# A bilinear feed-forward after sparse attention: two more pairs by seven products, another order at the end of a tile, banks by name

## The chip, the cores and the metric

The kernel runs on one core of a Trainium2 chip. The metric is the device time of one execution in microseconds. The engines are called as in the profile: PE multiplies matrices, PEld is its loading of weights, DVE, ACT and POOL work elementwise, SP issues transfers.

## The reference

```python
def _attn_ref(q, k, v):                     # q, k, v: (8, 8, 576, 64)
    scores = scale * np.matmul(q, k.transpose(0, 1, 3, 2))
    rel = pos[:, None] - pos[None, :]
    mask_local = (rel >= 0) & (rel < 32)
    mask_strided = (rel >= 0) & (pos[None, :] % 32 == pos[:, None] % 32)
    ...                                     # heads 0-3 local, 4-7 strided; softmax
    return np.matmul(attn, v)

def _moe_ref(x, w_a, w_b, w_out):           # x: 4608 x 512, w_a and w_b: 512 x 1536, w_out: 1536 x 512
    a = x @ w_a
    b = x @ w_b
    return (a * b @ w_out).astype(np.float32)

def reference(**kwargs):
    ...
    x = attn_out.transpose(0, 2, 1, 3).reshape(B * S, H * D)
    return _moe_ref(x=x, **moe_kwargs)
```

Only the second part, the feed-forward, is touched by the change. Its first projection is `a = x @ w_a` and `b = x @ w_b`, its second projection is `(a * b) @ w_out`.

## The kernel before

**Tiles and slots.** The 4,608 tokens are cut into nine tiles (`NT`, t = 0 to 8) of 512 (`TTOK`). Each tile has 16 slots: twelve for the blocks f of 128 columns of `d_ff` in the first projection (`ffn_ab`), then four for the second projection (`ffn_ys`, which draws 21 matmuls of a generator in each slot and the rest in the last). Blocks f = 2g and 2g + 1 are a pair; there are six pairs (`FG`), g = 0 to 5. The attention of the next batches is woven between these matmuls by `take`; the last of it is done within tile 6, so tiles 7 and 8 hold the feed-forward alone. Small works are hung on slots: `do(i, ...)` puts a call behind slot i, and the table `soon` does so ahead of `take(i)`. All five engines run in the order in which the program emits their instructions (`manual_schedule`).

**First projection, plain.** For one block f, `ab_mm` makes four matmuls of 512 columns for a and four for b (L626), each pair of banks from `mm_bank`. ACT copies a to `a_sb` (L647) and DVE multiplies it with b into `pf` (L650), as bf16.

**First projection, seven products.** For the pairs g listed in `FAST_A[t]` (in tiles 7 and 8), `a_pair` makes a of both blocks at once as a 2 x 2 block product by seven products instead of eight: the halves of the 512 contracted rows and the pair's two blocks on one side, the two halves of the tile's tokens on the other. The sums of weights (`wsum_make`) and of inputs (`xsum_make`) are made for all pairs ahead of time. Each product P("1") to P("7") is two matmuls of 256 columns (L703). Products 1, 6, 5, 3 accumulate in bank X, which ACT copies after each (L719, L722, L730, L738); 7 and 4 in bank Z, 2 in bank Y. ACT copies Z after product 7 (L725); DVE adds Y (L727) and Z (L736) to the quarters that they belong to, and POOL adds the copy of Z (L731). Between the products b is made plainly, four matmuls of 512 columns for each block (L710). `mult(1)` and then `mult(0)` multiply a with b for the odd and the even block (L715). The call is a generator with two parts, one for each of the pair's slots. X lies in the ring "st" for even g and "o" for odd g.

**Second projection.** In tiles 2 to 8 (`FAST_Y`) this is also made by seven products, with `pf` as the stationary side. `products(t)` says what each needs: product 1 the even blocks of `pf` and `w_out`, product 2 and 4 the odd blocks, 3, 5, 6 and 7 the differences s[0] to s[3] that `fast_s(t, n, gs)` makes from `pf` for the groups gs, n = 0 to 3 (L758, on DVE; product 6 needs n = 1, 7 needs n = 2, 5 needs n = 0, 3 needs n = 3, and n = 1 and 3 are made from n = 0 and 1). Each product is made for the two sets q = 0, 1 of tokens; a block such as "10" is product 1 for q = 0, six matmuls of 256 columns, one for each g. `Y_ORDER` (tiles 2 to 7, `y_plan`, L812) and `TAIL_ORDER` (tile 8, `y_tail`, L841) give the order of the 14 blocks. `y_post` takes a finished bank to `y_sb`: copies on ACT for products 1, 7, 6, 5 (L789) and 3 (L795), additions on DVE for 4 (L791) and 2 (L793), and one more on DVE after 5 (L787). In tile 8 the last block is cut in two halves of 128 columns, and `y_store` (L778) sends out the rows as they are done, five times through SP's queue and once through ACT's. In tile 7 the two stores (L807) hang on slots of tile 8.

**Tile 8's differences** are made group by group in the slots of its first projection. `fast_s` puts the difference n = 2 of a group off when this and the next pair are both in `FAST_A[8]`: `a_pair` of the next pair then makes it on POOL (`later`, L756, L733).

**Banks.** PSUM has eight: three in the ring "mm", one in "tp", and two each in "o" and "st". `mm_bank` counts its calls and takes "tp" at every fourth and "mm" otherwise; `a_pair` names its rings itself.

The order in time at the places that the change touches: pair 4 and pair 5 of tile 7, its second projection, pair 0 of tile 8, and so on up to pair 5 of tile 8, its second projection, and the last stores.

Of the kernel before, what the change touches and what calls it, by code (L numbers as in the profile page):

```python
# [7 lines left out]
F32 = mybir.dt.float32  # L8
# [16 lines left out]
VW = 128  # L25
WCH = (0, 2, 5, 9, 12)
FAST_Y = (2, 3, 4, 5, 6, 7, 8)
FAST_A = {7: (1, 2, 3, 4), 8: (0, 1, 2, 3, 4)}


@with_exitstack
def kernel(
# [571 lines left out]
    def take(pos):  # L604
        for b, names in steps.get(pos, ()):
            run(b, names)
# [5 lines left out]
    def mm_bank(shape):  # L612
        nm = "tp" if used[0] % 4 == 3 and used[0] >= 0 else "mm"
        used[0] += 1
        return psum4[nm].tile(shape, F32, tag=nm, name="mm")
# [65 lines left out]
    def a_pair(t, g):  # L681

        pf = pfs[t]
        pool, nm = ((pst, "st"), (psum4["o"], "o"))[g % 2]
        X = pool.tile([128, 2, 512], F32, tag=nm, name="ax")[:, 0, :HT]
        a = ([fsb.tile([128, TTOK], F32, tag="a_sb", name="a_sb") for _ in range(2)] if g % 2 == 0 else
             [t.rearrange("p h n -> p (h n)")[:, :2 * TTOK].bitcast(F32) for t in kT_buf[0]])
        got = {k: psum4[nm].tile([128, TTOK], F32, tag=nm, name="mm")
               for k, nm in zip((1, "Z", "Y", 0), (("mm", "mm", "tp", "mm"), ("tp", "mm", "mm", "mm"))[g % 2])}
        Z, Y = got["Z"][:, :HT], got["Y"][:, :HT]  # L690
        p7 = fsb.tile([128, HT], F32, tag="p7", name="p7")
        quarter = lambda e, k: a[e][:, HT * k:HT * (k + 1)]
        w = lambda e, j: (lambda c: wav[:, j, c, g, e])
        ws = lambda n: (lambda c: wsum_a[n][:, c, g])
        x = lambda j, k: (lambda c: x_part(t, j, k)[:, c])
        xs = lambda n: (lambda c: xsum[t][:, n, c])
        plan = {"1": (X, w(0, 0), x(0, 0)), "2": (Y, w(0, 1), x(1, 0)), "3": (X, ws(3), x(1, 1)), "4": (Z, w(1, 1), xs(3)),
                "5": (X, ws(0), xs(0)), "6": (X, ws(1), xs(1)), "7": (Z, ws(2), xs(2))}

        def P(k):  # L700
            bank, lhs, rhs = plan[k]
            for c in range(2):
                nc.tensor.matmul(bank, lhsT=lhs(c), rhs=rhs(c), start=k in "172" and c == 0, stop=c == 1, skip_group_check=True)  # L703

        x0 = TTOK * t % (XR * S)

        def b_mm(e, kks):
            f = 2 * g + e
            for kk in kks:
                nc.tensor.matmul(got[e], lhsT=wb_sb[:, kk, 128 * f:128 * (f + 1)], rhs=xT[:, kk, x0:x0 + TTOK],  # L710
                                 start=kk == 0, stop=kk == KD - 1)

        def mult(e):
            halves = lambda v_: v_.rearrange("p (a i s) -> p a i s", i=2, s=16)
            nc.vector.tensor_mul(pf[:, 2 * g + e, :].rearrange("p (i a s) -> p a i s", i=2, s=16),  # L715
                                 halves(a[e]), halves(got[e]))

        P("1")
        nc.scalar.copy(quarter(0, 0), X)  # L719
        b_mm(1, (0, 1, 2))  # L720
        P("6")
        nc.scalar.copy(quarter(1, 0), X)  # L722
        b_mm(1, (3,))
        P("7")
        nc.scalar.copy(p7, Z)  # L725
        P("2")
        nc.vector.tensor_tensor(quarter(0, 0), Y, quarter(0, 0), op=ALU.add)  # L727
        yield None
        P("5")
        nc.scalar.copy(quarter(1, 1), X)  # L730
        nc.gpsimd.tensor_tensor(quarter(1, 1), quarter(1, 1), p7, op=ALU.add)  # L731
        if (t, g - 1) in later:
            later.pop((t, g - 1))()  # L733
        b_mm(0, (0, 1))
        P("4")
        nc.vector.tensor_tensor(quarter(1, 0), Z, quarter(1, 0), op=ALU.add)  # L736
        P("3")
        nc.scalar.copy(quarter(0, 1), X)  # L738
        b_mm(0, (2, 3))
        mult(1)  # L740
        mult(0)
        yield pf[:1, 2 * g + 1, :1]

    later = {}
# [28 lines left out]
    def col(j):  # L773
        return slice(HN * j, HN * (j + 1))

    def y_store(eng, t, y, i, q, n=slice(0, d_model)):
        rows = out[TTOK * t:TTOK * (t + 1), n].rearrange("(a i s q) c -> a s i q c", i=2, s=8, q=2)
        eng.dma_start(out=rows[:, :, i, q], in_=y[i][:, q, n])  # L778
# [4 lines left out]
    def y_post(k, y, q, bank, n=slice(0, HN)):  # L783

        part = lambda i, j: y[i][:, q, HN * j:HN * (j + 1)]
        if k == "+":
            nc.vector.tensor_tensor(part(1, 1), part(1, 1), part(0, 1), op=ALU.add)  # L787
        elif k in "1765":
            nc.scalar.copy({"1": part(0, 0), "7": part(0, 1), "6": part(1, 0), "5": part(1, 1)}[k], bank)  # L789
        elif k == "4":  # L790
            nc.vector.tensor_tensor(part(1, 0), bank, part(1, 0), op=ALU.add)  # L791
        elif k == "2":
            nc.vector.tensor_tensor(y[0][:, q, n], bank, y[0][:, q, n], op=ALU.add)  # L793
        elif k == "3":
            nc.scalar.copy(part(0, 1), bank)  # L795

    Y_ORDER = [(x[0], int(x[1])) for x in "10 11 70 71 60 61 40 41 50 51 20 21 30 31".split()]
    TAIL_ORDER = [(x[0], int(x[1])) for x in "10 70 60 11 40 50 71 30 61 20 51 41 31 21".split()]

    def y_plan(t):  # L800

        plan, y = products(t), y_bufs()
        bank = {x: mm_bank([128, 2, HN]) for x in "ZXY"}

        def store_half(i):
            rows = out[TTOK * t:TTOK * (t + 1)].rearrange("(a i s q) c -> a s i (q c)", i=2, s=8, q=2)
            nc.sync.dma_start(out=rows[:, :, i], in_=y[i].rearrange("p q c -> p (q c)"))  # L807

        for n, (k, q) in enumerate(Y_ORDER):
            b, lhs, rhs = plan[k]  # L810
            for g in range(FG):
                nc.tensor.matmul(bank[b][:, q], lhsT=lhs(g, q), rhs=rhs(g), start=k in "172" and q == 0 and g == 0,  # L812
                                 stop=g == FG - 1, skip_group_check=True)
                if g == FG - 1:
                    if q == 1:
                        y_post(k, y, slice(0, 2), bank[b])
                        if k == "5":
                            y_post("+", y, slice(0, 2), None)
                    take(("y", t, n + 1))
                yield y  # L820
        do(16 * t + 19, store_half, 0)
        do(16 * t + 20, store_half, 1)

    def y_tail(t):

        plan, y = products(t), y_bufs()
        banks = [{x: mm_bank([128, HN]) for x in "ZXY"},
                 {"X": psum4["o"].tile([128, 2, 512], F32, tag="o", name="end")[:, 0, :HN],
                  "Z": pst.tile([128, 2, 512], F32, tag="st", name="end")[:, 0, :HN]}]
        for k, q in TAIL_ORDER:  # L830
            b, lhs, rhs = plan[k]
            cuts = [slice(0, HN)]
            if (q, k) == (1, "2"):
                cuts = [slice(0, 128), slice(128, HN)]
            for n in cuts:
                if (q, k) == (1, "2"):
                    bank = mm_bank([128, 128])
                else:
                    bank = banks[q][b]
                for g in range(FG):  # L840
                    nc.tensor.matmul(bank, lhsT=lhs(g, q), rhs=rhs(g)[:, n], start=g == 0 and k in "172",  # L841
                                     stop=g == FG - 1, skip_group_check=True)
                    if g < FG - 1:
                        yield y
                y_post(k, y, q, bank, n)
                if k == "5":
                    y_post("+", y, q, None)
                if k == "54"[q]:
                    y_store(nc.sync, t, y, 1, q)
                elif (q, k) == (0, "2"):  # L850
                    y_store(nc.sync, t, y, 0, q)
                elif (q, k) == (1, "3"):
                    y_store(nc.sync, t, y, 0, q, col(1))
                elif (q, k) == (1, "2"):
                    y_store(nc.scalar if n.start == 0 else nc.sync, t, y, 0, q, n)
                yield y

# [47 lines left out]
    with tc.manual_schedule(engines={ENG.PE, ENG.SP, ENG.Pool, ENG.DVE, ENG.Activation}):  # L905
# [88 lines left out]

        soon = {}
        for t in FAST_Y[:-1]:
            soon[16 * t + 10] = [lambda t=t: fast_s(t, 2, slice(4, 6))]
            soon[16 * t + 11] = [lambda t=t, n=n: fast_s(t, n, slice(4, 6)) for n in (0, 1)]
        do(0, fill_v, vl_buf[0])
        do(0, fill_v, vs_buf[0])  # L1000
# [40 lines left out]
        for n, slot in enumerate((16, 16, 19, 20)):  # L1041
            do(slot, fast_w, n, slice(3, 6))
        for g in range(FG):
            for n in (2, 0, 1, 3):
                do(16 * (NT - 1) + 2 * g + 1, fast_s, NT - 1, n, slice(g, g + 1))
        for t in FAST_Y[:-1]:
            for slot, n, z0, z1 in ((4, 0, 0, 2), (5, 2, 0, 2), (6, 1, 0, 2), (7, 3, 0, 2), (8, 2, 2, 4), (9, 0, 2, 4),
# [45 lines left out]
```

## Time and profile before

| | us |
|---|---|
| median of 3 runs | 325.69 (325.45 to 326.91) |
| the profiled execution | 325.6 |
| span of its profile, first to last instruction | 323.9 |
| tile 7, pair 0 (plain), 260.92 to 264.37 | 3.45 |
| tile 7, pairs 1 to 4 (seven products), 264.37 to 277.39 | 13.02 |
| tile 8, pair 0 (seven products), 290.03 to 293.51 | 3.48 |
| tile 8, pairs 1 to 4 (seven products), 293.51 to 306.53 | 13.02 |

The time of an execution lies 1.7 us above the span of its profile. In the rows of busy time by stretch, as the next section shows them, a row gives the stretch in microseconds from the span's start, its length, and then for PE, PEld, DVE, ACT and POOL the busy time and the number of instructions that lie in it, wholly or in part; the last three numbers are the granted clock of PE, the share of the DMA engines' time and GB/s. In the rows of the order of time, the first two numbers are the start and the length of a group of instructions, followed by engine, line, operation, what it writes and reads, the shape and the count; a bracket holds the idle time before and who ended it. A matmul's record is longer than its share of PE, since matmuls overlap; what counts is the distance from start to start.

### The profile page before, as it was taken

Reading aid. Unit: us, or ns where it says so; the run is one execution under the profiler, and the core shown is the slowest. Engines: PE = TensorE matmul, PEld = TensorE weight load, DVE = VectorE, ACT = ScalarE, POOL = GpSimd, SP = SyncE. Lnnn points to the kernel's source line nnn. Section 1 sums busy time; section 2 is a strip of 40 time slices with the busy share of each in tenths; the row PEclk is TensorE's granted clock in tenths of the full one; section 3 lists DMA queues with packets and bytes.
Section 4 is the critical chain, followed back from the end, with each engine's and each line's share of the span. In section 5 each row is a group of like instructions: output and inputs, shape, how many; then the busy total and the mean of one; then the engine's idle time right before and its main releaser. Section 6 shows DMA issues by size and latency. Waiting matters only on the chain.

```text
span 323.9 us, 7466 instructions
## 1 busy us (share of the span) xinstructions
PE 317.7 (98%) x2686; PEld 209.2 (65%) x2686; DVE 258.6 (80%) x560; ACT 189.4 (58%) x332; POOL 161.0 (50%) x291
## 2 busy tenths in 40 slices
PE   8999999999999999999999999999999999999994
PEld 6754655455555587557999885569555966686673
DVE  6766888888778899898888888988999768837952
ACT  6764775478764576447644764476546655335541
POOL 8935848599857554853576247634013012203500
PEclk9999999999999999999999999999999999999999
DMA  9999999999999989999999999999146040004004
GB/s 158 151 203 194 204 187 188 170 174 129 141 216 142 134 87 98 111 209 152 101 101 189 176 97 106 175 194 115 33 95 157 10 130 3 0 0 132 1 2 130
DMA packets 110724, 40.43 MB, mean 125 GB/s; under 512 B 88672, under 2 KB 107744, under 8 KB 110688
## 3 DMA queue, kind: packets, MB, share of 16 engines
q0 software_dynamic: 85968, 19.48, 67.0%
q1 hardware_dynamic: 24576, 20.42, 25.1%
q8 instruction: 21, 0.34, 0.5%
q14 instruction: 15, 0.12, 0.1%
q10 hardware_dynamic: 144, 0.07, 0.1%
HBM read 39.51 MB, written 10.91 MB: 156 GB/s over the span
## 4 chain that ended last, share of the span: by engine, by line
PE 95%; DMA 1%; ACT 1%; DVE 1%; issue 0%; SPq 0%
PE mm L626 46%; PE mm L812 17%; PE mm L876 6%; PE mm L710 5%; PE st L392 4%; PE o L470 2%; PE ax L703 2%; PE o L529 2%; PE mm L703 2%; PE mm L841 2%; PE end L841 1%; DMA raw<-in_q_dram 1%; PE misc L155 1%; PE ab L626 1%; PE tp L296 1%; PE tp L554 1%
## 5 line engine op out<-in xcount | busy, mean ns | idle before, releaser
L626 PE MATMUL mm<-xT,wa_sb 128*128 128x512 bf16 (+1 forms) x400 | 92.6, 353 | 0.0
L626 PE MATMUL mm<-xT,wb_sb 128*128 128x512 bf16 (+1 forms) x400 | 92.6, 353 | 0.0
L647 ACT COPY a_sb<-mm 128x512 f32<-128x512 f32 x88 | 51.4, 585 | 51.3 <-PE mm L626 49.3
L626 PEld LDWEIGHTS <-wb_sb 128*128 128x128 bf16 x408 | 39.4, 98 | 35.6 <-DMA wb_sb<-in_moe_w_b_dram 0.2
L1059 POOL CAST pace<-pf 1x1 f32<-1x1 bf16 x83 | 24.7, 298 | 69.0 <-DVE pf L650 48.3
L626 PEld LDWEIGHTS <-wa_sb 128*128 128x128 bf16 x408 | 36.6, 98 | 23.1 <-issue 0.2
L650 DVE TENSOR_TENSOR pf<-a_sb,mm 128x512 bf16<-128x512 f32 x66 | 44.8, 680 | 8.4 <-PE mm L626 7.2
L413 ACT ACTIVATE p<-st 72x576 bf16<-72x576 f32 (+1 forms) x56 | 36.4, 650 | 14.4 <-PE st L392 14.2
L545 DVE TENSOR_TENSOR xT<-o,xr 64x288 bf16<-64x288 f32 x48 | 21.4, 446 | 14.7 <-ACT xr L539 14.4
L812 PEld LDWEIGHTS <-ps 128*128 128x128 bf16 x288 | 28.0, 98 | 3.1
L789 ACT COPY y_sb<-mm 128x512 f32<-128x512 f32 (+1 forms) x28 | 15.5, 555 | 17.9 <-PE mm L812 15.3
L812 PE MATMUL mm<-wf,ps 128*128 128x256 bf16 x216 | 25.5, 273 | 0.0
L538 ACT ACTIVATE xr<-o 64x576 f32<-64x576 f32 x28 | 18.1, 647 | 12.0 <-PE o L529 11.7
L876 PE MATMUL mm<-wo_sb,pf 128*128 128x512 bf16 x96 | 23.4, 379 | 0.0
L243 POOL DMA_DIRECT2D vs<-in_v_dram x24 | 19.6, 818 | 5.0 <-PE mm L812 2.4
L812 PEld LDWEIGHTS <-pf 128*128 128x128 bf16 x216 | 20.3, 98 | 2.5 <-issue 0.2
L1059 POOL COPY pace<-y_sb 1x1 f32<-1x1 f32 x23 | 5.0, 217 | 33.2 <-DVE y_sb L787 19.8
L710 PE MATMUL mm<-xT,wb_sb 128*128 128x512 bf16 x72 | 21.4, 379 | 0.0
L539 ACT ACTIVATE xr<-xr 64x576 f32<-64x576 f32 x28 | 19.1, 683 | 0.9
L812 PE MATMUL mm<-wo_sb,pf 128*128 128x256 bf16 x144 | 18.5, 273 | 0.1
L212 POOL DMA_DIRECT2D kl<-in_k_dram x24 | 16.1, 672 | 4.8 <-issue 3.2
L212 POOL DMA_DIRECT2D ql<-in_q_dram x24 | 15.9, 664 | 5.0 <-DMA wo_sb<-in_moe_w_out_dram 3.9
(189 smaller groups left out, 574.4 us busy)
## 6 DMA issues: line engine op xcount, KB each, us to landing
out_dram<-y_sb SPq DMA_DIRECT2D x12, 512.0 KB, 5.0
out_dram<-y_sb SPq DMA_DIRECT2D x11, 256.0 KB, 3.6
vl<-in_v_dram POOLq DMA_DIRECT2D x6, 384.0 KB, 8.2
kl<-in_k_dram POOLq DMA_DIRECT2D x24, 72.0 KB, 3.3
ql<-in_q_dram POOLq DMA_DIRECT2D x24, 72.0 KB, 3.3
vs<-in_v_dram POOLq DMA_DIRECT2D x24, 72.0 KB, 4.3
wo_sb<-in_moe_w_out_dram POOLq DMA_DIRECT2D x4, 384.0 KB, 9.2
natk<-in_k_dram POOLq DMA_DIRECT2D x20, 72.0 KB, 3.5
```

The lines of the kernel that those rows point to most:

```text
L212: nc.gpsimd.dma_start(out=t[32 * h:32 * h + 32], in_=src[b, h].rearrange("(i y) d -> y i d", y=32))
L243: nc.gpsimd.dma_start(out=vs_buf[b % 2][:, h, :, 0:D], in_=v[b, HL + h].rearrange("(p r) d -> p r d", r=RS))
L413: nc.scalar.activation(p_flat(p)[:M, :2 * W].rearrange("p (i n) -> p i n", n=2 * n), st[:M].rearrange("p a (i n) -> p (a i) n", n=256)[:, ...
L539: nc.scalar.activation(r, r, ACT.Exp, scale=-1.0)
L545: nc.vector.tensor_mul(dst.rearrange("d (p r) -> d p r", r=RS)[:, :, G * half:G * (half + 1)], o[:64, j, :W].rearrange("d (g p) -> d p g", ...
L626: nc.tensor.matmul(ps_[:, c0:c0 + n], lhsT=w[:, kk, 128 * f:128 * (f + 1)], rhs=xT[:, kk, x0:x0 + n], start=(kk == first and c0 == 0), sto ...
L647: nc.scalar.copy(a_sb, ab[0])
L650: nc.vector.tensor_mul(pf[:, f, :].rearrange("p (i a s) -> p a i s", i=2, s=16), halves(a_sb), halves(ab[1]))
L710: nc.tensor.matmul(got[e], lhsT=wb_sb[:, kk, 128 * f:128 * (f + 1)], rhs=xT[:, kk, x0:x0 + TTOK], start=kk == 0, stop=kk == KD - 1)
L812: nc.tensor.matmul(bank[b][:, q], lhsT=lhs(g, q), rhs=rhs(g), start=k in "172" and q == 0 and g == 0, stop=g == FG - 1, skip_group_check=True)
L876: nc.tensor.matmul(ybank[j], lhsT=pf[:, f, 128 * j:128 * (j + 1)], rhs=wo_sb[:, f], start=(f == 0), stop=(f == FD - 1))
L1059: nc.gpsimd.tensor_copy(pace, done)
```

## The change

`FAST_A` gets pair 5 in both tiles, so that all pairs of tile 8 and all but the first of tile 7 make a by seven products. In the last pair of a tile, `mult(0)` comes ahead of `mult(1)`, in tile 7 with the difference n = 2 of groups 4 and 5 between them (it leaves `soon`). In tiles 7 and 8 the second projection's matmuls are ordered by `by_block`: the first two blocks make their groups 0 to 4 first, then group 5 of each; the other blocks follow as before. `TAIL_ORDER` is another order of the same blocks, and the stores of tile 8 follow other blocks for q = 0. The banks of the second projection in tiles 7 and 8 are asked for by ring (`bank_of`) instead of by `mm_bank`'s count. In tile 8 the differences are made in the order n = 0, 1, 2, 3. Tiles 0 to 6 keep their order of work.

```diff
@@ -25,7 +25,7 @@
 VW = 128
 WCH = (0, 2, 5, 9, 12)
 FAST_Y = (2, 3, 4, 5, 6, 7, 8)
-FAST_A = {7: (1, 2, 3, 4), 8: (0, 1, 2, 3, 4)}
+FAST_A = {7: (1, 2, 3, 4, 5), 8: (0, 1, 2, 3, 4, 5)}
 
 
 @with_exitstack
@@ -737,8 +737,14 @@
         P("3")
         nc.scalar.copy(quarter(0, 1), X)
         b_mm(0, (2, 3))
-        mult(1)
-        mult(0)
+        if g < FG - 1:
+            mult(1)
+            mult(0)
+        else:
+            mult(0)
+            if t < NT - 1:
+                fast_s(t, 2, slice(4, 6))
+            mult(1)
         yield pf[:1, 2 * g + 1, :1]
 
     later = {}
@@ -795,63 +801,73 @@
             nc.scalar.copy(part(0, 1), bank)
 
     Y_ORDER = [(x[0], int(x[1])) for x in "10 11 70 71 60 61 40 41 50 51 20 21 30 31".split()]
-    TAIL_ORDER = [(x[0], int(x[1])) for x in "10 70 60 11 40 50 71 30 61 20 51 41 31 21".split()]
+    TAIL_ORDER = [(x[0], int(x[1])) for x in "10 11 20 60 70 61 50 71 30 40 51 41 31 21".split()]
+
+    def by_block(order, lead):
+
+        head = order[:lead]
+        return [(k, q, g) for k, q in head for g in range(FG - 1)] + [(k, q, FG - 1) for k, q in head] + [
+            (k, q, g) for k, q in order[lead:] for g in range(FG)]
+
+    def bank_of(nm, shape):
+        return psum4[nm].tile(shape, F32, tag=nm, name="mm")
 
     def y_plan(t):
 
         plan, y = products(t), y_bufs()
-        bank = {x: mm_bank([128, 2, HN]) for x in "ZXY"}
+        late = t in FAST_A
+        if late:
+            bank = {x: bank_of(nm, [128, 2, HN]) for x, nm in (("X", "mm"), ("Z", "mm"), ("Y", "tp"))}
+        else:
+            bank = {x: mm_bank([128, 2, HN]) for x in "ZXY"}
 
         def store_half(i):
             rows = out[TTOK * t:TTOK * (t + 1)].rearrange("(a i s q) c -> a s i (q c)", i=2, s=8, q=2)
             nc.sync.dma_start(out=rows[:, :, i], in_=y[i].rearrange("p q c -> p (q c)"))
 
-        for n, (k, q) in enumerate(Y_ORDER):
+        for k, q, g in by_block(Y_ORDER, 2 if late else 0):
             b, lhs, rhs = plan[k]
-            for g in range(FG):
-                nc.tensor.matmul(bank[b][:, q], lhsT=lhs(g, q), rhs=rhs(g), start=k in "172" and q == 0 and g == 0,
-                                 stop=g == FG - 1, skip_group_check=True)
-                if g == FG - 1:
-                    if q == 1:
-                        y_post(k, y, slice(0, 2), bank[b])
-                        if k == "5":
-                            y_post("+", y, slice(0, 2), None)
-                    take(("y", t, n + 1))
-                yield y
+            nc.tensor.matmul(bank[b][:, q], lhsT=lhs(g, q), rhs=rhs(g), start=k in "172" and q == 0 and g == 0,
+                             stop=g == FG - 1, skip_group_check=True)
+            if g == FG - 1:
+                if q == 1:
+                    y_post(k, y, slice(0, 2), bank[b])
+                    if k == "5":
+                        y_post("+", y, slice(0, 2), None)
+                take(("y", t, Y_ORDER.index((k, q)) + 1))
+            yield y
         do(16 * t + 19, store_half, 0)
         do(16 * t + 20, store_half, 1)
 
     def y_tail(t):
 
         plan, y = products(t), y_bufs()
-        banks = [{x: mm_bank([128, HN]) for x in "ZXY"},
-                 {"X": psum4["o"].tile([128, 2, 512], F32, tag="o", name="end")[:, 0, :HN],
-                  "Z": pst.tile([128, 2, 512], F32, tag="st", name="end")[:, 0, :HN]}]
-        for k, q in TAIL_ORDER:
+        banks = {("X", 1): psum4["o"].tile([128, 2, 512], F32, tag="o", name="end")[:, 0, :HN],
+                 ("Z", 1): pst.tile([128, 2, 512], F32, tag="st", name="end")[:, 0, :HN]}
+        for x in "XYZ":
+            banks[x, 0] = bank_of("mm", [128, HN])
+        for k, q, g in by_block(TAIL_ORDER, 2):
             b, lhs, rhs = plan[k]
-            cuts = [slice(0, HN)]
-            if (q, k) == (1, "2"):
-                cuts = [slice(0, 128), slice(128, HN)]
-            for n in cuts:
-                if (q, k) == (1, "2"):
-                    bank = mm_bank([128, 128])
-                else:
-                    bank = banks[q][b]
-                for g in range(FG):
+            last = (k, q) == TAIL_ORDER[-1]
+            if last and g:
+                continue
+            for n, nm in ((slice(0, 128), "tp"), (slice(128, HN), "mm")) if last else ((slice(0, HN), None),):
+                bank = bank_of(nm, [128, 128]) if last else banks[b, q]
+                for g in range(FG) if last else (g,):
                     nc.tensor.matmul(bank, lhsT=lhs(g, q), rhs=rhs(g)[:, n], start=g == 0 and k in "172",
                                      stop=g == FG - 1, skip_group_check=True)
                     if g < FG - 1:
                         yield y
+                if g < FG - 1:
+                    continue
                 y_post(k, y, q, bank, n)
                 if k == "5":
                     y_post("+", y, q, None)
-                if k == "54"[q]:
+                if k == "4":
                     y_store(nc.sync, t, y, 1, q)
-                elif (q, k) == (0, "2"):
-                    y_store(nc.sync, t, y, 0, q)
-                elif (q, k) == (1, "3"):
-                    y_store(nc.sync, t, y, 0, q, col(1))
-                elif (q, k) == (1, "2"):
+                elif k == "3":
+                    y_store(nc.sync, t, y, 0, q, slice(0, d_model) if q == 0 else col(1))
+                elif last:
                     y_store(nc.scalar if n.start == 0 else nc.sync, t, y, 0, q, n)
                 yield y
 
@@ -994,7 +1010,8 @@
 
         soon = {}
         for t in FAST_Y[:-1]:
-            soon[16 * t + 10] = [lambda t=t: fast_s(t, 2, slice(4, 6))]
+            if t not in FAST_A:
+                soon[16 * t + 10] = [lambda t=t: fast_s(t, 2, slice(4, 6))]
             soon[16 * t + 11] = [lambda t=t, n=n: fast_s(t, n, slice(4, 6)) for n in (0, 1)]
         do(0, fill_v, vl_buf[0])
         do(0, fill_v, vs_buf[0])
@@ -1041,7 +1058,7 @@
         for n, slot in enumerate((16, 16, 19, 20)):
             do(slot, fast_w, n, slice(3, 6))
         for g in range(FG):
-            for n in (2, 0, 1, 3):
+            for n in range(4):
                 do(16 * (NT - 1) + 2 * g + 1, fast_s, NT - 1, n, slice(g, g + 1))
         for t in FAST_Y[:-1]:
             for slot, n, z0, z1 in ((4, 0, 0, 2), (5, 2, 0, 2), (6, 1, 0, 2), (7, 3, 0, 2), (8, 2, 2, 4), (9, 0, 2, 4),
```

## The prediction

> **What bounds the kernel now.** I read the busy shares first, then the busy time by stage over the last two tiles (the only ones the change touches), then the chain that ended last, then the order of time at the two seams, and the transfers of the last 13 us.
>
> ```profile
> PE 317.7 (98%) x2686; PEld 209.2 (65%) x2686; DVE 258.6 (80%) x560; ACT 189.4 (58%) x332; POOL 161.0 (50%) x291
> ```
> ```profile
> 274.14:277.39 3.25, 3.25 (x23) 2.10 (x22) 2.79 (x7) 1.89 (x6) 0.91 (x2) 1.00 0.02 5
> 277.39:280.85 3.46, 3.46 (x19) 1.62 (x17) 3.06 (x6) 1.17 (x2) 0.54 (x2) 1.00 0.00 0
> 280.85:290.03 9.18, 9.18 (x86) 8.22 (x85) 5.46 (x11) 2.35 (x4) 1.04 (x3) 1.00 0.00 0
> ...
> 306.53:310.08 3.55, 3.55 (x19) 1.65 (x18) 2.95 (x7) 1.17 (x2) 0.71 (x2) 1.00 0.00 0
> 310.08:319.31 9.23, 9.21 (x91) 8.06 (x88) 4.00 (x11) 3.72 (x10) 0.31 (x1) 1.00 0.21 53
> 319.31:323.90 4.59, 0.00 (x0) 0.00 (x0) 0.29 (x1) 0.00 (x0) 0.00 (x0) 1.00 0.45 126
> ```
> TensorE is the bound: each stage's PE busy time is its length, at a granted clock of 1.00. The rows are tile 7's pair 4 (seven products), its pair 5 (plain) and its second projection, then tile 8's pair 5 (plain), its second projection, and the end after the last matmul. What is worth reading is therefore PE's instruction time, every wait of PE, and the 4.59 us in which only stores run.
>
> ```profile
> 280.68 1.47 PE L812 MATMUL mm<-wo_sb,pf 128*128 128x256 bf16 x12
> ...
> 305.94 0.59 PE L710 MATMUL mm<-xT,wb_sb 128*128 128x512 bf16 x2
> 306.47 1.02 PE L626 MATMUL mm<-xT,wa_sb 128*128 128x512 bf16 x4
> ```
> ```profile
> 305.99 0.42 DVE L736 TENSOR_TENSOR a_sb<-mm,a_sb 128x256 f32<-128x256 f32 x1
> 306.52 1.28 DVE L715 TENSOR_TENSOR pf<-a_sb,mm 128x512 bf16<-128x512 f32 x2
> ...
> 310.19 0.69 DVE L650 TENSOR_TENSOR pf<-a_sb,mm 128x512 bf16<-128x512 f32 x1 [0.61 <-PE mm L626]
> ```
> Two matmuls of 512 columns from 305.94 should be followed at 306.37; the next starts at 306.47, 0.06 after the addition of L736 ended (306.41). That is a bank wait of 0.10 us, and 0.06 is what a hand-over costs. The last row: the multiplication of a finished bank starts 0.27 after PE's next matmul has started (309.92), and takes 0.69.
>
> **Removed work: the pairs.** A plain pair is 16 matmuls of 512 columns, 3.46 us (0.216 each). A seven-product pair is 8 of 512 (1.73) and 14 of 256 at 0.109 (1.52): 3.25, as its row shows. That is -0.20 us for tile 7, and -0.20 for tile 8, where the same step from start to start is 3.45 (306.47 to 309.92). The bank wait at 306.47 goes too: the pair's first product now writes the other ring ("ax"), whose copies are long done: -0.10. The weight loads (22 of 0.098, 2.15 us) stay under the 3.25 of streaming.
>
> By the Trainium skill ("TensorE: Matmul & The Clock Gate", section Back-to-back issue gap) a sustained stream spends some 131 ns on a matmul of 512 columns and 81 on one of 128; an estimate between them, 98 ns for 256, would make 14 short products (1.37 us) dearer than 8 long ones (1.05), and the change 0.65 us slower over both pairs. The rows here say 216 and 109, so the trace is against it.
>
> **Added work off PE.** Per pair ACT gets 5 copies of 0.37 for 2 of 0.585 (1.86 for 1.17), DVE two additions of 0.42, POOL one addition of 0.73. They lie under PE as in the neighbour pair, whose row has DVE at 2.79 and ACT at 1.89 of 3.25; without that cover the 0.84 of DVE would be the price. In tile 8 the difference n=2 of group 4 moves from DVE (0.29) to POOL (0.67), behind POOL's addition. By tile 8's own rhythm it ends some 0.6 after the second projection's start; product 7 needs that group at +3.06. The order n = 0, 1, 2, 3 puts difference 2 of group 5 third; covered below.
>
> **Moved work: the seams.** Let T be the start of the first matmul of the second projection. DVE's new wait is mult(0) on the end of the b products; behind it in DVE's queue stand the differences and mult(1), and behind those PE's products. With spacings from the rows (0.69 a multiplication, next start 0.61 later where independent; 0.42 a difference over two groups; 0.29 over one; 0.04 between dependents):
> Tile 7: mult(0) T+0.27 to 0.96, difference 2 to 1.42, mult(1) 1.34 to 2.02, difference 0 to 2.48, difference 1 to 2.94. PE does ten products of the first five groups before it needs mult(0), at T+1.09 (ready 0.96+0.06 = 1.02); product 7 needs group 4 at T+1.75 (1.48); product 6 at T+3.06 (3.00). No stall, but only 0.07 and 0.06 of slack, where the old order had over 1.1 at product 6. If DVE is later by d, PE loses d less 0.06; with the old order of blocks mult(0) would be needed at T+0.55, a stall of 0.47.
> Tile 8: mult(1) ends T+1.56 (needed 1.85), difference 1 at 2.22 (needed 2.51), difference 2 at 2.43 (needed 3.17). No stall; the old 0.03 at the first product 7 (310.57 to 311.91 for 12 products, 1.34 for 1.31) goes.
> Banks: L626 took, at 306.47, the bank that L736 freed, the earliest freed of its ring, not the one allotted first, which a multiplication still read until 307.2. By that, X of both second projections gets the bank of Y of pair 5, freed over a microsecond before: no wait. Were banks handed round in turn, X would get that of Z, and PE would wait 0.10 in tile 7 and 0.10 in tile 8. I take 0, and keep 0 to +0.20. A gain beyond is excluded: 84 products of 0.109 fill the 9.18 of tile 7.
> Tile 7 into 8: P6 starts at 290.96, not at the 290.72 its three b products end at, held by ACT's copy L719 behind L795. Neither moves against PE: the 0.24 stays.
>
> **Moved stores.** SP still issues five, ACT one. The first moves from behind block 50 to block 30, so SP's first two are 0.7 apart, not 2.25:
>
> ```profile
> DMA  0000000000002978100298829899881000000000
> GB/s 0 0 0 0 0 0 0 0 0 0 0 0 69 195 183 309 51 0 0 76 195 195 309 82 189 170 340 366 238 224 36 0 0 0 0 0 0 25 0 0
> ```
> A character is 0.325 us from 312. The stores issued at 314.93 and 317.18 each move 256 KB in 1.3 us, beginning 1.0 after their issue; those of 318.54 on move 512 KB in 2.05. An issue holds SP 0.54. With PE 0.53 earlier, the first two are issued at 315.88 and 316.58 and the third at 318.01, with data due about 319.1. One after another at 1.3 they end at 316.85+2.6 = 319.45: +0.35; packed as the closing ones, at 318.9: 0. I take +0.1, nearer the packed row, since they follow as closely. The last chain (two half blocks, DVE 0.29, store) is as before.
>
> **Sum.** -0.20 -0.20 -0.10 -0.03 + 0 + 0.1 = -0.43 against the profiled execution of 325.6 (span 323.9): 325.2. Its median of three is 325.69, 0.09 above; between, I forecast **325.3 us**. Anything within 0.5% (1.6 us, 324.06 to 327.32) is about what a measurement here can't tell from no change, so this counts as no change.
>
> **Rivals.**
> *The seams eat the gain* (15%): DVE is 0.2 late at each of the two tight spots and banks go round in turn: 2 x 0.14 + 0.20 = +0.48, so 325.7. For it: 0.06 of slack and DVE at 80%. Against: these spacings repeat to 0.01 from pair to pair.
> *The crowded stores decide* (8%, slower than before): the first two 256 KB stores delay the third. It decides once a store takes over 1.39 us of the engines (316.85 + 2 x 1.39 = 319.63, eating the whole 0.53). Stores of this size earlier in the kernel land after 3.6 us, not 2.8; 0.5 of that 0.8 makes 1.8 a store, 320.45, a delay of 1.35, and 326.4; all of it 327.0. Against: those ran beside loads, and here nothing else moves.
> *Short products are held by their weights* (2%): if the six more loads of a pair (0.098) lay open, 12 x 0.098 = 1.18 would make 326.4. Against: the row of 3.25. The sustained figures of the Trainium skill that are cited above (section Back-to-back issue gap) stand on this side, with 0.65 for 1.18, and the trace does not bear them out.
> *It does not do what it says* (5%): the seven-product pair waits for DVE as last pair and takes 3.45 again; 325.7.
>
> **How the numbers follow.** The forecast has 70%. Bounds: -0.53 with no cost at the stores, +0.02 with +0.35 there and +0.20 in banks: 325.1 to 325.6 on the profiled execution. The three runs lie from 325.45 to 326.91, so a median can be half a microsecond off: 324.5 to 326.4 holds forecast, seams, no saving and the lower half of the crowded stores. Slower by over 0.5% needs the worst of those stores plus an unlucky median or a wait I don't see: 6%. Faster by over 0.5% needs 1.6 us where 0.53 is on offer: 3%. No change: 91%.
>
> **What would show it.** Pair 5 of both tiles at 3.25 with 22 loads; the first L703 after 305.94 at 306.37; the second projections still 9.18, with the product after the first 10 no later than T+1.09; DVE's L715 for the even block first, at T+0.27; SP's first two stores under a microsecond apart, the last DMA activity 2.3 us after the last matmul. A second projection of 9.3 or more, or a gap in PE at product 6, would make the seams right; a third store landing after more than 3.2 us, the stores. A time outside 324.5 to 326.4 would say that something else moved, in tiles 0 to 6, whose order of work the change leaves alone.

## The result, and the profile after

| | before | after |
|---|---|---|
| median of 22 runs each, us | 326.44 (325.45 to 331.39) | 325.46 (324.82 to 327.69) |
| ratio of after to before, 95% interval | | 0.9974 (0.9964 to 0.9984) |
| span of the profile, us | 323.9 | 324.3 |

The ratio is a gain of 0.85 us (0.52 to 1.17) on 326.44. It lies within the 0.5% that the forecast called no change; 22 runs of each make it plain all the same. The forecast of 325.3 is 0.16 off the median, but that is in part luck: the three runs it started from had a median of 325.69, the 22 have 326.44, and from that base the foretold gain of 0.43 would have given 326.0. A base that was too low and a gain that was too small made up for each other.

The span of the changed kernel's profile is longer, not shorter. The chain of waits of its first 60 us has a line that the profile of before does not have (start, length, what):

```profile
14.49 14.60 DMA wb_sb<-in_moe_w_b_dram
```

PE waited in tile 0 for weights. Its first seven-product matmul in tile 7 starts at 265.39, against 264.21 in the kernel before: 1.18 us lost before anything that the change touches. Taken weight load by weight load, PE is 0.58 us behind the kernel before at 14.6, 1.14 at 33 and 1.19 from 85 us to tile 7: the loss belongs to the start, and about half of it to the time of this wait. So the two profiles are compared from that matmul on. Busy time by stage of the changed kernel, columns as before (length; PE, PEld, DVE, ACT, POOL busy and instructions; clock, DMA share, GB/s):

```profile
278.58:281.83 3.25, 3.25 (x24) 2.15 (x23) 2.79 (x6) 1.83 (x5) 0.92 (x2) 1.00 0.00 0
281.83:291.02 9.19, 9.19 (x87) 8.24 (x85) 6.49 (x13) 2.38 (x5) 0.69 (x3) 1.00 0.01 2
...
307.50:310.77 3.27, 3.27 (x24) 2.17 (x23) 2.92 (x7) 1.83 (x5) 1.54 (x4) 1.00 0.00 0
310.77:319.98 9.21, 9.19 (x91) 8.15 (x88) 4.51 (x12) 3.67 (x11) 0.85 (x2) 1.00 0.19 55
319.98:324.30 4.32, 0.00 (x0) 0.00 (x0) 0.29 (x1) 0.00 (x0) 0.00 (x0) 0.92 0.47 131
```

The rows are the counterparts of those of before: pair 5 of tile 7 (3.46, now 3.25), its second projection (9.18, now 9.19), pair 5 of tile 8 (3.55, now 3.27), its second projection (9.23, now 9.21), the end (4.59, now 4.32). Both pairs gave what was foretold, the second projections gave nothing back, and the end is shorter by 0.27 (by 0.22 with spans to the nanosecond, 323.889 and 324.341), which no step of the forecast had.

Order of time at tile 7's seam in the changed kernel, PE and then DVE (start, length, instructions):

```profile
281.24 0.59 PE L710 MATMUL mm<-xT,wb_sb 128*128 128x512 bf16 x2
281.67 1.47 PE L830 MATMUL mm<-wo_sb,pf 128*128 128x256 bf16 x12
282.98 2.78 PE L830 MATMUL mm<-wf,ps 128*128 128x256 bf16 x24
285.60 1.47 PE L830 MATMUL mm<-wf,pf 128*128 128x256 bf16 x12
```
```profile
281.29 0.42 DVE L736 TENSOR_TENSOR kT0s<-mm,kT0s 128x256 f32<-128x256 f32 x1
281.93 0.69 DVE L715 TENSOR_TENSOR pf<-kT0l,mm 128x512 bf16<-128x512 f32 x1 [0.21 <-ACT kT0l L738]
282.65 0.42 DVE L764 TENSOR_TENSOR ps<-pf 128x512 bf16<-128x512 bf16 x1
282.99 0.68 DVE L715 TENSOR_TENSOR pf<-kT0s,mm 128x512 bf16<-128x512 f32 x1
283.70 0.42 DVE L764 TENSOR_TENSOR ps<-pf 128x512 bf16<-128x512 bf16 x1
284.16 0.42 DVE L764 TENSOR_TENSOR ps<-ps,pf 128x512 bf16<-128x512 bf16 x1
```

With T = 281.67, PE's 12 products of block 10 and 11 take 1.31 and the 24 behind them 2.62 from start to start: no gap. DVE's even multiplication starts at T+0.26, difference 2 at +0.98, the odd multiplication at +1.32, difference 1 ends at +2.91; foretold were +0.27, +1.00, +1.34 and +2.94. PE starts 0.43 after the last two b matmuls, although the addition L736, which reads Z's bank, ends only at 281.71: X was not given that bank.

Transfers from 312.7 on, each character 0.325 us:

```profile
DMA  0000000000000000079899639799880000000000
GB/s 0 0 0 0 25 0 0 0 0 0 0 0 0 0 0 0 0 158 164 277 397 334 265 88 195 176 344 356 227 227 19 0 0 0 0 0 0 0 0 0
```

The two stores that now follow each other closely (issued at 317.11 and about 317.8) have moved their 512 KB by 320.2, in some 1.9 us: packed, not one after the other at 1.3. The third, issued at 319.21, begins 1.0 later as if alone.

### The profile page after: what moved, and what is told of

Same layout as the page of the kernel before. It is cut to its first block, busy times and chain, and to the rows that moved or that the text cites. A ratio compares the mean times of both kernels' runs of the same rounds, so it can differ in the third digit from the quotient of the medians.

```text
span 324.3 us, 7477 instructions
## 1 busy us (share of the span) xinstructions
PE 316.7 (98%) x2669; PEld 211.2 (65%) x2698; DVE 259.9 (80%) x563; ACT 190.9 (59%) x338; POOL 162.7 (50%) x293
## 4 chain that ended last, share of the span: by engine, by line
PE 88%; DMA 5%; POOL 4%; DVE 1%; issue 1%; ACT 1%; POOLq 0%
PE mm L626 42%; PE mm L830 17%; PE mm L892 6%; PE mm L710 5%; DMA wb_sb<-in_moe_w_b_dram 5%; PE st L392 4%; PE ax L703 3%; PE mm L703 2%; PE o L529 2%; PE o L470 2%; PE mm L857 2%; POOL shared L197 1%; PE end L857 1%; POOL wa_sb L252 1%; POOL vl L225 1%
## 5 line engine op out<-in xcount | busy, mean ns | idle before, releaser
L626 PE MATMUL mm<-xT,wb_sb 128*128 128x512 bf16 (+1 forms) x381 | 88.2, 352 | 0.7 <-DMA wb_sb<-in_moe_w_b_dram 0.4
L626 PE MATMUL mm<-xT,wa_sb 128*128 128x512 bf16 (+1 forms) x367 | 86.6, 351 | 0.8
L647 ACT COPY a_sb<-mm 128x512 f32<-128x512 f32 x84 | 49.2, 586 | 47.6 <-PE mm L626 45.6
L626 PEld LDWEIGHTS <-wb_sb 128*128 128x128 bf16 x392 | 37.8, 98 | 34.3 <-DMA wb_sb<-in_moe_w_b_dram 1.1
L626 PEld LDWEIGHTS <-wa_sb 128*128 128x128 bf16 x392 | 35.1, 98 | 21.1
L650 DVE TENSOR_TENSOR pf<-a_sb,mm 128x512 bf16<-128x512 f32 x62 | 42.1, 679 | 7.3 <-PE mm L626 6.1
L795 ACT COPY y_sb<-mm 128x512 f32<-128x512 f32 (+1 forms) x28 | 15.6, 556 | 17.6 <-PE mm L830 15.0
L710 PE MATMUL mm<-xT,wb_sb 128*128 128x512 bf16 x83 | 25.3, 379 | 0.1
L652 DVE TENSOR_TENSOR pf<-a_sb,mm 128x512 bf16<-128x512 f32 x22 | 14.9, 677 | 4.8 <-ACT a_sb L647 2.7
```

What stands on the lines that cost most here:

```text
L626: nc.tensor.matmul(ps_[:, c0:c0 + n], lhsT=w[:, kk, 128 * f:128 * (f + 1)], rhs=xT[:, kk, x0:x0 + n], start=(kk == first and c0 == 0), sto ...
L647: nc.scalar.copy(a_sb, ab[0])
L650: nc.vector.tensor_mul(pf[:, f, :].rearrange("p (i a s) -> p a i s", i=2, s=16), halves(a_sb), halves(ab[1]))
```

## The experiments

For every run the table gives the time from the first seven-product matmul of tile 7 (L703) to the end of the last addition on DVE (L793, L799 or L795), the rest of the span after that (from spans to the nanosecond; the expectations took spans to 0.1, so their 4.28 and 4.01 stand for 4.27 and 4.05 in the table), and the ratio to runs of the kernel before that were taken beside it. The expectations of the first two experiments used the chain's start of that matmul, 0.16 later than its record, so their 55.25 and 54.73 stand for 55.41 and 54.89 in the table.

| kernel | to the last addition, us | end, us | ratio, 95% interval |
|---|---|---|---|
| before | 55.42 | 4.27 | |
| before, again | 55.41 | 4.24 | 1.0001 (0.9992 to 1.0009) |
| after | 54.90 | 4.05 | 0.9974 (0.9964 to 0.9984) |
| after, again | 54.90 | 4.02 | 0.9974 (0.9959 to 0.9989) |
| pairs alone | 56.81 | 4.12 | 1.0051 (1.0037 to 1.0066) |
| seams alone | 55.30 | 4.25 | 0.9993 (0.9981 to 1.0006) |
| blocks whole | 55.84 | 4.05 | 1.0017 (1.0002 to 1.0032) |
| odd block first | 55.73 | 4.03 | 1.0012 (1.0002 to 1.0023) |
| banks by count | 57.27 | 4.07 | 1.0058 (1.0041 to 1.0075) |
| stores late | 54.90 | 4.03 | 0.9983 (0.9971 to 0.9996) |
| tile 7 only | 55.09 | 4.04 | 0.9986 (0.9977 to 0.9995) |
| tile 8 only | 55.09 | 4.05 | 0.9980 (0.9969 to 0.9991) |
| stores behind | 54.89 | 5.59 | 1.0027 (1.0015 to 1.0038) |
| copy on DVE | 54.65 | 4.03 | 0.9967 (0.9955 to 0.9980) |

The first column repeats to 0.01 us for the same order of work, where whole runs scatter by a microsecond or more: in these 14 profiles the first seven-product matmul starts anywhere from 264.07 to 265.61. That column is what the mechanisms are judged by; the ratio says whether the whole agrees.

**Both kernels once more.** No edit.

> The kernel before, run against itself, to see what the start and the end of a profile scatter by. Ratio 1.000 within its interval. Theory A (the gain is PE's 0.53 us in the last two tiles; the 0.27 us that the time from the last DVE addition to the end of the span fell by, 4.28 to 4.01, is scatter): here the end takes anything from 4.0 to 4.3 us. Theory B (the other order of stores shortens the end): here the end takes 4.28 again, within 0.05. From the first L703 of tile 7's pair 1 to the last DVE addition's end both expect 55.25 us.

> The changed kernel once more. Theory A: from tile 7's pair 1 to the last addition's end 54.73 us as in its first profile, 0.52 under the kernel before, the end anywhere from 4.0 to 4.3 us, ratio 0.9984 (0.53 of 326). Theory B: the end at 4.0 us again, ratio 0.9975 (0.8 us).

The touched stretch falls by 0.51 again. The end is 4.24 and 4.02: lower by 0.22, as it was in the first two profiles (4.27 and 4.05), so this is more than scatter. What part of it differs is seen in the waits of SP in the last 12 us (who waited for whom; us in total, times, longest). The kernel before, again, and then the changed one, again:

```profile
SPq L1088 <- PEq L1088: 0.9, 2, 0.7
```
```profile
SPq L1105 <- PEq L1105: 0.7, 2, 0.5
```

The wait for the last store is 1.8 in both. Behind it SP waits twice more, for the other engines, at the line that ends the program, and the second of these waits is 0.2 shorter now. The view names PE's sequencer, but the instructions of that line name another engine. Each engine's last drain (an instruction that counts up the semaphore on which POOL waits before it lets all go on) is in these rows: count, ns of the shortest, median and longest, first and last start. The kernel before, again, and then the changed one, again:

```profile
L1088 PEldq DRAIN  x2: 13/752/1490, 318.4 to 323.8; - x2
L1088 DVEq DRAIN  x2: 145/238/330, 319.9 to 324.1; - x2
```
```profile
L1105 PEldq DRAIN  x2: 13/748/1482, 318.5 to 323.8; - x2
L1105 DVEq DRAIN  x2: 19/174/330, 320.0 to 323.8; - x2
```

In the kernel before DVE's last drain starts at 324.1, behind that of PE's sequencer (PEldq) at 323.8, and takes 145 ns; in the changed one both start at 323.8, and DVE's takes 19 ns. So it is DVE that comes last, and PE is not late.

**The pairs without the rest.** The kernel before with

```diff
-FAST_A = {7: (1, 2, 3, 4), 8: (0, 1, 2, 3, 4)}
+FAST_A = {7: (1, 2, 3, 4, 5), 8: (0, 1, 2, 3, 4, 5)}
...
-            soon[16 * t + 10] = [lambda t=t: fast_s(t, 2, slice(4, 6))]
-            soon[16 * t + 11] = [lambda t=t, n=n: fast_s(t, n, slice(4, 6)) for n in (0, 1)]
+            if t not in FAST_A:
+                soon[16 * t + 10] = [lambda t=t: fast_s(t, 2, slice(4, 6))]
+            soon[16 * t + 11] = [lambda t=t, n=n: fast_s(t, n, slice(4, 6)) for n in ((2, 0, 1) if t in FAST_A else (0, 1))]
```

> The kernel before with pair 5 of tiles 7 and 8 by seven products and nothing else of the change (difference 2 of tile 7 is made after the pair's multiplications, which it needs). Theory A: the pairs give 0.20 + 0.20 + 0.10, but block 10 needs the even multiplication 0.55 us into the second projection and gets it at 1.49, a stall of 0.94 in each tile; sum +1.4 us against before, ratio 1.004. Rival (the seams hide nothing): the stalls stay away and the kernel is as fast as the changed one, ratio 0.998.

56.81 is 1.39 above before, for 1.4 foretold, and the kernel is slower by 0.5%. The 0.5 us saved at the pairs is worth nothing without the seams: in the last pair both multiplications come at the end, and block 10 needs the second one. PE at tile 7's seam:

```profile
281.23 0.71 PE L812 MATMUL mm<-wo_sb,pf 128*128 128x256 bf16 x5
282.72 0.94 PE L812 MATMUL mm<-wo_sb,pf 128*128 128x256 bf16 x7 [0.78 <-DVE pf L715]
```

Five products of 0.109 from 281.23 should be followed at 281.78, and are at 282.72: 0.94, as foretold.

**The seams without the pairs.** The changed kernel with

```diff
-FAST_A = {7: (1, 2, 3, 4, 5), 8: (0, 1, 2, 3, 4, 5)}
+FAST_A = {7: (1, 2, 3, 4), 8: (0, 1, 2, 3, 4)}
...
-            if t not in FAST_A:
+            if FG - 1 not in FAST_A.get(t, ()):
                 soon[16 * t + 10] = [lambda t=t: fast_s(t, 2, slice(4, 6))]
```

> The changed kernel with pair 5 of both tiles plain again: new order of blocks, of stores and of banks, no seven products in the last pairs. Theory A: pairs back at 3.45 us; the bank wait of 0.10 at tile 8's pair 5 goes since the count of banks gives it another ring, so -0.1 us against before, ratio 0.9997. Theory B: the end at 4.0 us, -0.4 us, ratio 0.9988.

55.30, 0.12 below before: the bank wait of 0.10 and the 0.03. The last b matmuls ahead of tile 8's pair 5 start at 305.80 and the next one at 306.23, 0.43 later, where the kernel before took 0.53. The end is 4.25 and SP's last waits are 0.9 again, with the new order of stores in place. That is against Theory B: the order of stores did not shorten the end.

**Each piece of the seam taken out.** Three kernels, each the changed one with one piece undone:

```diff
-        for k, q, g in by_block(Y_ORDER, 2 if late else 0):
+        for k, q, g in by_block(Y_ORDER, 0):
...
-        for k, q, g in by_block(TAIL_ORDER, 2):
+        for k, q, g in by_block(TAIL_ORDER, 0):
```

> The changed kernel, with every block of the second projection made in one go (groups 0 to 5 of block 10 before block 11), in tiles 7 and 8. Theory A: product 10 needs group 5 at T+0.55 and the even multiplication is there at T+1.02 (T: start of the second projection), a stall of 0.47 us in each tile; first L703 of pair 1 to the end of the last addition 54.90 + 0.94 = 55.84. Rival (the late group hides nothing, PE has other slack): 54.90 again.

```diff
-        if g < FG - 1:
-            mult(1)
-            mult(0)
-        else:
-            mult(0)
-            if t < NT - 1:
-                fast_s(t, 2, slice(4, 6))
-            mult(1)
+        mult(1)
+        mult(0)
+        if g == FG - 1 and t < NT - 1:
+            fast_s(t, 2, slice(4, 6))
```

> The changed kernel with the old order of the two multiplications in the last pair (odd block, even block, and difference 2 after both). Theory A: the odd one waits for POOL's addition until about T+0.15, the even one ends at T+1.43 and reaches PE at 1.49, needed at T+1.09: a stall of 0.40 in each tile, 54.90 + 0.80 = 55.70. Rival (the odd one is done before the b products end, so order does not matter): at most 0.05 in each tile.

```diff
-        if late:
-            bank = {x: bank_of(nm, [128, 2, HN]) for x, nm in (("X", "mm"), ("Z", "mm"), ("Y", "tp"))}
-        else:
-            bank = {x: mm_bank([128, 2, HN]) for x in "ZXY"}
+        bank = {x: mm_bank([128, 2, HN]) for x in "ZXY"}
...
-        for x in "XYZ":
-            banks[x, 0] = bank_of("mm", [128, HN])
+        for x in "ZXY":
+            banks[x, 0] = mm_bank([128, HN])
```

> The changed kernel with the banks of the second projections of tiles 7 and 8 drawn by the running count again. Theory A: the count now gives the ring with one bank to Z in tile 7 and to X in tile 8, and that bank is freed by the odd multiplication: tile 7's product 7 waits from T+1.31 to T+2.08 (0.77), tile 8's first product from T to T+1.62 (1.62). Sum 54.90 + 2.4 = 57.3. Rival (banks do not matter, only the order of blocks does): 54.90 to 55.1.

Measured 55.84, 55.73 and 57.27, for 55.84, 55.70 and 57.3. The order of time of PE shows the waits where they were foretold; the bracket gives the idle time and who ended it. Blocks whole, tile 7:

```profile
280.94 0.71 PE L830 MATMUL mm<-wo_sb,pf 128*128 128x256 bf16 x5
281.95 0.94 PE L830 MATMUL mm<-wo_sb,pf 128*128 128x256 bf16 x7 [0.29 <-DVE pf L715]
```

Odd block first, tile 7:

```profile
281.15 1.26 PE L826 MATMUL mm<-wo_sb,pf 128*128 128x256 bf16 x10
282.65 0.39 PE L826 MATMUL mm<-wo_sb,pf 128*128 128x256 bf16 x2 [0.24 <-DVE pf L715]
```

Banks by count, tile 7's product 7 and tile 8's first product:

```profile
281.88 1.47 PE L827 MATMUL mm<-wo_sb,pf 128*128 128x256 bf16 x12
283.94 2.80 PE L827 MATMUL mm<-wf,ps 128*128 128x256 bf16 x24 [0.58 <-DVE pf L715]
...
313.19 0.72 PE L854 MATMUL mm<-wo_sb,pf 128*128 128x256 bf16 x5 [1.44 <-DVE pf L715]
```

A bracket is 0.17 to 0.18 shorter than the real delay, because a matmul's record outlasts its share of PE. From starts: five products of 0.109 from 280.94 should be followed at 281.48, and are at 281.95 (0.47); ten from 281.15 at 282.24, and are at 282.65 (0.41); twelve from 281.88 at 283.19, and are at 283.94 (0.75). In tile 8 of the last kernel two b matmuls from 311.15 should be followed at 311.58, and are at 313.19 (1.61, for 1.62 foretold). All have L715, a multiplication, as releaser: in the first two kernels for its result, in the last one because it reads the bank that the count hands to the next product.

**One tile at a time.** The changed kernel with pair 5 by seven products in one tile only (and the condition on `soon` of the seams alone):

```diff
+FAST_A = {7: (1, 2, 3, 4, 5), 8: (0, 1, 2, 3, 4)}     # tile 7 only
+FAST_A = {7: (1, 2, 3, 4), 8: (0, 1, 2, 3, 4, 5)}     # tile 8 only
```

> The changed kernel with pair 5 by seven products in tile 7 only, plain in tile 8. Theory A: 0.20 us of PE time under the kernel with both pairs plain (55.30), 55.10 from pair 1's first L703 to the end of the last addition. For the 0.2 us by which the last wait on PE's sequencer fell (0.9 to 0.7 in every kernel with both pairs, whatever its order of stores): if it hangs on the last tile's pair it is 0.9 here and 0.7 in the sister run with tile 8 only; if it hangs on the length of PE's program (24 rows more with both pairs, 12 with one), it need not be so, and one value for both sister runs speaks for that.

> The changed kernel with pair 5 by seven products in tile 8 only, plain in tile 7. Theory A: 55.10 here too, 0.20 under the kernel with both pairs plain. The last wait on PE's sequencer: 0.7 if it hangs on the last tile's pair, the same as in the sister run if it hangs on the length of PE's program.

55.09 in both, 0.21 under the seams alone: the pairs are worth the same and add up. SP's last waits are 0.7 in both, so they do not hang on the last tile's pair. In all 14 profiles they go with DVE's last drain. In the three profiles without a seven-product pair 5 (DVE has 560 instructions there, by the first lines of their pages) the drain starts 0.44 to 0.45 us after the end of DVE's instruction ahead of it; in the eleven others (561 to 564) it starts 0.09 after it. What holds DVE up is not shown. One thing goes with it in every profile: the last load of 8 KB on the DMA queue q14, of the kind "instruction", starts 0.3 us after the end of the span in those three, and 8 to 12 us ahead of it in the eleven. It is the lone 25 in the rows of GB/s, at 324.2 in the kernel before and at 314.2 in the changed one. That DVE waits there for its program's next piece is a guess that no run tested.

**Stores.** The first attempt moved only the place in the program at which the stores of q = 0 are issued:

```diff
+                if (k, q) == ("4", 1):
+                    y_store(nc.sync, t, y, 0, 0)
+                    y_store(nc.sync, t, y, 1, 0)
+                    y_store(nc.sync, t, y, 1, 1)
```

> The changed kernel with the two 256 KB stores for q = 0 of tile 8 held back to just ahead of that for q = 1 (all three behind block 41). Theory A (the stores of q = 0 have room where the change put them; the DMA engines take 256 KB in 1.0 to 1.3 us when packed): 1 MB from about 1.0 after the first issue, 4.1 to 4.6 us, so it ends 1.6 to 2.1 us later than now and the end after the last addition grows from 4.0 to 5.6 or 6.1. Rival (the end is all latency of the last small store): 4.0 again, or 0.2 more for SP's queue.

It tested nothing: SP's order stays the same, each store waits only for its own rows, and the first was issued at 317.04, before block 41 was done. It is a third run of the changed kernel (54.90, 4.03, ratio 0.9983). The second attempt puts them behind in SP's own queue, `y_store` of (1, 1) ahead of (0, 0) and (1, 0):

> The changed kernel with the two 256 KB stores for q = 0 of tile 8 put behind that of q = 1 in SP's queue, so that they are issued after block 41. Theory A (the DMA engines take 256 KB in 1.0 to 1.3 us when packed, SP 0.64 to issue one): the last small store is issued 1.3 later and 1 MB takes 4.1 us from about 1.0 after the first issue; the end after the last addition grows from 4.0 to between 5.3 and 6.1. Rival (the stores have so much room that their place is free): 4.0 to 4.3.

The end grows to 5.59, by 1.5. Transfers from 312.9 on, 0.325 us a character:

```profile
DMA  0000000000000000000000899999999981000000
GB/s 0 0 25 0 0 0 0 0 0 0 0 0 0 0 0 0 0 0 0 0 0 0 183 176 309 391 302 381 276 268 320 306 262 54 0 0 0 0 0 0
```

1 MB goes in one piece of 3.6 us, near 290 GB/s on the mean, and the last small store is issued 1.4 later (321.5). In this place the stores decide the end. In the changed kernel they have room: the first two are through by 320.2, when the third begins.

**A version without the wait at tile 8's start.** The forecast left a wait of 0.24 at tile 8's start untouched. In the changed kernel (order of time, PE and ACT):

```profile
290.84 0.38 PE L703 MATMUL ax<-xT,wa_sb 128*128 128x256 bf16 x2
291.04 0.59 ACT L801 COPY y_sb<-mm 128x512 f32<-128x512 f32 x1 [2.03 <-PE mm L830]
...
291.52 0.38 ACT L719 COPY a_sb<-ax 128x256 f32<-128x256 f32 x1
...
291.95 0.38 PE L703 MATMUL ax<-qz1s,vl 128*128 128x256 bf16 x2
```

L719 frees the bank of product 6 and queues behind the last copy of tile 7. In tile 7 that copy goes to DVE (`y_post` gets a parameter `dve`, False by default):

```diff
...
-            nc.scalar.copy(part(0, 1), bank)
+            (nc.vector.tensor_copy if dve else nc.scalar.copy)(part(0, 1), bank)
...
-                    y_post(k, y, slice(0, 2), bank[b])
+                    y_post(k, y, slice(0, 2), bank[b], dve=late)
```

> The changed kernel with the copy of product 3 in tile 7's second projection on DVE, which is idle there, and not on ACT. Theory A: PE's wait of 0.24 us at tile 8's first product 6, which ACT's copy of 512 columns holds up, goes; 54.90 - 0.24 = 54.66, ratio against before 0.9967 where the changed kernel has 0.9974. Rival (something else holds product 6, the bank of b or the sums of inputs): 54.90.

```profile
289.94 0.38 PE L703 MATMUL ax<-xT,wa_sb 128*128 128x256 bf16 x2
290.14 0.69 DVE L801 COPY y_sb<-mm 128x512 f32<-128x512 f32 x1 [0.38 <-PE mm L830]
...
290.36 0.37 ACT L719 COPY a_sb<-ax 128x256 f32<-128x256 f32 x1 [2.25 <-PE ax L703]
...
290.80 0.38 PE L703 MATMUL ax<-qz1s,vl 128*128 128x256 bf16 x2
```

Product 6 starts 0.86 after product 1 and no longer 1.11, the stretch is 54.65 for 54.66 foretold, and the median is 325.08 beside 326.1 for the kernel before: 0.9967 (0.9955 to 0.9980). That interval overlaps the changed kernel's (0.9964 to 0.9984); that this version is faster than the changed one is shown by the stretch, 0.25 shorter in one profile, not yet by whole runs.

## Why the prediction was right, and where it was short

**The pairs: right.** 0.20 and 0.20 were foretold; the two runs with one tile each give 0.21 and 0.21 against the seams alone. The sustained figures that the forecast cited from the Trainium skill ("TensorE: Matmul & The Clock Gate", section Back-to-back issue gap) would have made each pair dearer by 0.32; the stages of 3.25 and 3.27 decide against them here, and with them falls the rival that short products are held by their weights.

**The bank wait and the small stall: right.** -0.13 foretold, -0.12 in the seams alone. In the changed kernel no bank wait takes their place, which agrees with the reading that a ring hands out the bank freed first; at tile 7's seam X was plainly not given the bank freed last.

**The seams: right, and the reason holds.** DVE's times were met to 0.04. The slack of 0.06 at product 6 was enough; difference 1 ended at T+2.91 and product 6 needs it at T+3.06. Each of the three pieces is needed: without it the wait that its price was worked out for appears, 0.47, 0.41 and 0.75 in tile 7. The rival that the seams eat the gain is out for the changed kernel; it describes the pairs alone.

**The wait at tile 8's start: right.** It stayed at 0.24, and the copy on DVE shows that its cause was read rightly.

**The stores: mis-sized.** The term taken was +0.1, between 0 and +0.35; it measured 0. The first two stores packed at 512 KB in 1.9 us, which was the lower bound's row. The rival of the crowded stores is a real mechanism, 1.5 us when they are queued behind, but the changed kernel does not reach the point from which it decides.

**The last chain: wrong in size.** "As before" was the step: the time after the last addition fell by about 0.2 in every kernel with a seven-product pair 5 (the stores behind aside), because DVE's last drain is no longer late at the line that ends the program. Nothing in the forecast had a price for that, and the expectations that named PE's sequencer had the wrong engine. Why DVE was late stays open.

The traced sum is -0.52 and about -0.2, -0.7, where -0.43 was foretold and -0.85 (0.52 to 1.17) measured. The rest of 0.15 is inside the interval; the forecast's 0.43 lies just outside it, by the two terms above.

## What to carry to other kernels

Compare two profiles from the first instruction of the touched stretch, not by their spans: here the span rose by 0.4 us while the stretch fell by 0.52, because the first 85 us differed by more than the change is worth. When arithmetic is saved right ahead of a hand-over, work out when each operand is there and when PE first asks for it: 0.5 us saved in the pairs became 1.4 us lost until the last group was asked for later, its multiplication came first, and the banks came from tiles that were freed early. To put a store off, change its place in its queue; its place in the program alone does nothing.

## What the hardware showed that was not expected

The end of the program depends on something besides the last store: DVE's last drain was 0.44 to 0.45 us behind its instruction before in the three profiles without a seven-product pair 5 and 0.09 in the eleven with one, whatever the order of work, and SP's last two waits were 0.9 and 0.7 us. A view that names the releaser of such a wait can name the wrong engine; the starts of the instructions of that line showed the late one. The DMA engines took stores of 256 KB at 1.3 us each when apart, 1.9 for two when close, and 3.6 for 1 MB in one piece: in these three cases, the more was queued, the nearer to 290 GB/s.
